# Linear attention feeding a squared-ReLU layer: two blocks of attention handled as one, and first blocks' steps at other places

## Chip, cores and metric

One core of one Trainium2 chip. The metric is the device time of one launch in microseconds (us), median of several runs of the same program; lower is better. TensorE is called PE, VectorE DVE, ScalarE ACT, GpSimd POOL, and SyncE SP; nearly all DMAs are issued from SP's queue.

## What is computed

Cut to what matters:

```python
# q, k, v, alpha: (4, 8, 768, 48)   w_in: (384, 2048)   w_out: (2048, 384)
for t in range(S):
    state = alpha[:, :, t, :, None] * state + einsum('bhd,bhe->bhde', k[:, :, t], v[:, :, t])
    y[:, :, t] = einsum('bhd,bhde->bhe', q[:, :, t], state)
x = y.transpose(0, 2, 1, 3).reshape(B * S, H * D)      # 3072 x 384
h = maximum(x @ w_in, 0)
out = (h * h) @ w_out
```

The first part is linear attention with a decay for each key feature, in sequence over 768 steps; the second is a feed-forward layer on its output. The weights come as 64-bit floats and are made into 32-bit ones on the chip.

## The kernel before

The sequence is cut into six chunks of 128 steps. A block is one chunk of one batch, so there are 24 blocks; block n has chunk n // 4 and batch n % 4. Four blocks make a group, and the 512 rows of x that a group gives go through the feed-forward layer together. Six groups are passed in turn (the program's g, 0 to 5), and while PE works on the layer of group g, the attention of group g + 1 is put in between.

**Attention of a block.** The logs of alpha (`ln`, on ACT) are summed along the chunk by a matmul with a triangular matrix (`cs`); from block 8 on the log is split on DVE into a high and a low part of fewer bits each (`sp`), so that this matmul runs in two fast passes. The exponentials of the sums and of their negatives (`eb`, `ei`, on ACT) scale q and k (`mq`, `mk`, on DVE). PE transposes both (`turn`, tile `T`), ACT copies them out of PSUM (`kc`, `qc`). Then `scores` (k with q, in two halves of 64 steps) and `state_sums` (k with v) write into the same two PSUM banks (tile `sckv`, lines L418 and L441). On DVE, `masked` copies the scores under a triangular mask into `am` (L426), `sums_copied` adds the old state to the first half's sums (`us`, L452), and `next_state` adds the second half's (L466) and multiplies by the last row of decays (L467). That row has to be turned from a row into a column: `bl` writes it to DRAM (`row<-b`), and `br` reads it back in two DMAs (`last<-row`). Output y is made in two parts, the first in `ga` (`yq` from states, and half of the masked scores), the second in `gb`; `ev` copies it out of PSUM to x.

**Pairs.** From block 4 on, work is placed by pairs n, n + 1. `PLAN` and `EARLY` (L996 to L1016) give each step of a pair a due time, in units of PE work, where 1.05 stands for six matmuls of 512 columns; `weave` (L1052) puts a step in front of the first piece of the layer that begins at or after its time. In `ga` of pair n: scores, sums, mask and us of block n, first part of y of pair n - 2, state step of block n. In `gb`: second part of y of pair n - 2, then scores, sums, mask, us and state step of block n + 1. Loads of later blocks are issued from the same plan, when the tile that they overwrite has been read. The table `AT` (L19) holds due times, scales and switches.

**The layer.** In group 0, and partly in group 1, it is computed with plain 32-bit matmuls (`h<-x,w_in`, `o<-w_out,hid`). After that each operand is split into a coarse part and a rest, and each product is made in three faster passes: in `in_x` the coarse one (`h<-xa,wb`) and the rests (`h<-xl,wl`), in `in_y`, two pieces later, a third with differences (`h<-xd,wd`). `in_post` makes the squared ReLU, `split_h` and `diff_h` split it for the second matmul. The split weights are made once (`prepare`), kept in DRAM, and streamed in again for every group (`pump`, as long as fewer than `room` tiles are in use). `split_x` and `diff_x` split the group's x, for each of three slices of 128 rows.

**The start.** An order written out by hand (`first`, L980 to L989) holds blocks 0 to 3, loads and weights among it. `warm` and `zeros` (L243, L380) are matmuls whose result nobody reads. `first0`, `middle0`, `second0` convert weight chunk 0 from 64 to 32 bits, on DVE (L174, L178), ACT (L187, L190) and DVE (L196, L200, L203). A word such as `gy0` holds the next load back until a mark has passed, here the first part of y of blocks 0 and 1.

All PSUM tiles come from one pool of eight banks. Every engine runs its own instructions in the order in which the program gives them.

Of the kernel before, what the change touches and what calls it, by code (L numbers as in the profile page):

```python
# [17 lines left out]
GB = 4  # L18
AT = {'u0': 2, 'evs': 0.4, 'lead': 4, 'post': 3, 'w_first': (45.82, 44.44, 94.99), 'wstep': 2.31, 'w_in_at': 1.92, 'w_in_by': 3.02, 'room1': 25, 'room': 26, 's0': 3, 'ahead': 12, 'late': 23, 'xs': 0.35, 'g0': (-0.17, 20.59, 27.02), 'sc0': (2.36, 2.26, 2.42), 'g1': (7.68, 18.74, 27.21), 'g': (2.3, 15.42), 'g1x': 47.42, 'gx': 39.86, 'g0x': 55.51, 'k0': 2, 'h0': 16, 'k1': 5, 'h1': 0, 'h1by': 5, 'evs0': 0.23, 'tp': 'DDAD', 'tp1': 'AADD', 'split': 8, 'o0': (42.39, 46.35), 'o1': (), 'o2': (21.54, 19.65, 30.49, 26.1, 43.38, 50.96), 'str1': 14.0, 'ga': 9.32, 'gb': 12.97}  # L19
# [6 lines left out]
def kernel(  # L26
# [37 lines left out]
    s_all = kept("s", B + 2, [128, NP, 64])  # L64
    u_all = kept("us", 3, [128, NP, 64])
    for t in s_all[0:B]:
        nc.gpsimd.memset(t, 0.0)
    s_t = [s_all.pop(0) for _ in range(B)]
    NV = 4
    tiles = {  # L70
        "a": kept("a_in", 2, [128, H * D]), "q": kept("q_in", 2, [128, H, 64]),
        "k": kept("k_in", 3, [128, H, 64]), "v": kept("v_in", NV, [128, H * D]),
    }
    for t in tiles["q"] + tiles["k"]:
        nc.gpsimd.memset(t[:, :, D:64], 0.0)

    NW = 8
    wt_pool = ctx.enter_context(tc.tile_pool(name="wt", bufs=26))
# [16 lines left out]
    for x, n in (("q", 2), ("q", 3), ("k", 3)):  # L95
        t = lent[x, n] = two_k("qk_lent", shape=(H, 64))
        nc.gpsimd.memset(t[:, :, D:64], 0.0)

    def tile_of(x, n):
        return lent.get((x, n), tiles[x][n % len(tiles[x])])  # L100
# [11 lines left out]
    marks, held = {}, []  # L112

# [12 lines left out]
    def load(n, xs="aqkv"):  # L126
        c, b = divmod(n, B)
        for x in xs:
            t = dense.get((x, n), tile_of(x, n))
# [62 lines left out]
    def convert_second(i):  # L192
# [10 lines left out]
        nc.vector.tensor_tensor(out=w, in0=w, in1=power.bitcast(FP32), op=ALU.mult)  # L203

# [27 lines left out]
    for t in s_all + u_all:  # L232
        nc.gpsimd.memset(t, 0.0)
# [4 lines left out]
    rows_t = [dram.tile([1, H * D], FP32, name=f"row{n}") for n in range(NBLK)]  # L238
# [4 lines left out]
    def warm(_):  # L243
        nc.tensor.matmul(
            out=ps_att.tile([128, NP, 64], FP32, tag="att", name="warm"),
            lhsT=s_t[0].rearrange("a p d -> a (p d)")[:, 0:128], rhs=s_t[0], start=True, stop=True,
        )

    for _ in range(3):
        warm(0)  # L250

# [13 lines left out]
    def ln(n):  # L265
        la = blk[n]["la"] = tile_of("a", n)
        nc.scalar.activation(out=la, in_=la, func=AF.Ln)

    SPLIT = AT["split"]

    def sp(n):
        if n < SPLIT:
            return
        la = blk[n].pop("la")
        hi = p2.tile([128, H * D], FP32R, tag="b", name="hi")
        lo = p2.tile([128, H * D], FP32R, tag="inv", name="lo")
        nc.vector.tensor_copy(out=hi, in_=la)
        nc.vector.tensor_tensor(out=lo, in0=la, in1=hi.bitcast(FP32), op=ALU.subtract)  # L280
        blk[n]["parts"] = hi, lo

    def cs(n):

        ps = blk[n]["cs"] = bank(n, "cs")
# [10 lines left out]

    def eb(n):
        if n < GB:
            b = blk[n]["b_wide"] = b_wide[n]
            b = blk[n]["b"] = b[:, :, 0:D]  # L300
            sums = sums_of_logs(n).rearrange("a (h d) -> a h d", h=H)
            nc.scalar.activation(out=b, in_=sums, func=AF.Exp)
            return
        b = p2.tile([128, H * D], FP32, tag="b", name="b")
        nc.scalar.activation(out=b, in_=sums_of_logs(n), func=AF.Exp)
        b = blk[n]["b"] = b.rearrange("a (h d) -> a h d", h=H)

    def ei(n):
        inv = blk[n]["inv"] = p2.tile([128, H * D], FP32, tag="inv", name="inv")
# [849 lines left out]
```

## Time and profile before

| | before |
|---|---|
| runs, median of 3 (lowest, highest) | 516.7 us (516.4, 516.85) |
| the profiled execution: span from first to last instruction | 514.6 us |
| granted TensorE clock | 1.00 |
| HBM read, written | 84.57 MB, 17.33 MB |
| DMA engines, mean share | 71% |

The page gives for the profiled execution its span; a launch's time has 2.1 us more in the median of the runs. In the rows of the profile L12 is line 12 of the kernel, "x24" a count, and `out<-in` names the tiles. Rows of the chain of waits give start, length and what; rows of the timeline give start, length, engine, line, operation, and in brackets the idle time in front of it with what ended it. Rows of groups give the busy time, a comma, the mean of one in ns, and then idle time in front. An instruction of 32-bit matmul stands as two records.

### The profile page before, as it was taken

Reading aid. Unit: us, or ns where it says so; the run is one execution under the profiler, and the core shown is the slowest. Engines: PE = TensorE matmul, PEld = TensorE weight load, DVE = VectorE, ACT = ScalarE, POOL = GpSimd, SP = SyncE. Lnnn points to the kernel's source line nnn. Section 1 sums busy time; section 2 is a strip of 40 time slices with the busy share of each in tenths; the row PEclk is TensorE's granted clock in tenths of the full one; section 3 lists DMA queues with packets and bytes.
Section 4 is the critical chain, followed back from the end, with each engine's and each line's share of the span. In section 5 each row is a group of like instructions: output and inputs, shape, how many; then the busy total and the mean of one; then the engine's idle time right before and its main releaser. Section 6 shows DMA issues by size and latency. Waiting matters only on the chain.

```text
span 514.6 us, 12773 instructions
## 1 busy us (share of the span) xinstructions
PE 508.3 (99%) x5166; PEld 404.6 (79%) x5166; DVE 377.0 (73%) x656; ACT 302.3 (59%) x627; POOL 6.0 (1%) x33
## 2 busy tenths in 40 slices
PE   8999999999999999999999999999999999999997
PEld 6884456669877679988888888888888888888996
DVE  3798899898789869886698286799275588274961
ACT  4789875677788576376764175855075663144520
POOL 4000000000000000000000000000000000000000
PEclk9999999999999999999999999999999999999999
DMA  9989867272797788799975678894775544789201
GB/s 171 226 238 269 233 177 226 33 224 101 267 238 199 189 188 234 263 330 222 241 187 154 209 220 229 222 225 146 227 221 168 186 128 151 214 277 401 88 0 63
DMA packets 144794, 102.73 MB, mean 200 GB/s; under 512 B 116560, under 2 KB 118240, under 8 KB 144736
## 3 DMA queue, kind: packets, MB, share of 16 engines
q1 hardware_dynamic: 144736, 101.92, 70.4%
q8 instruction: 41, 0.67, 0.6%
q14 instruction: 17, 0.14, 0.1%
HBM read 84.57 MB, written 17.33 MB: 198 GB/s over the span
## 4 chain that ended last, share of the span: by engine, by line
PE 96%; DMA 2%; SPq 1%; DVE 1%; issue 0%; ACT 0%; DVEq 0%; POOLq 0%
PE h L681 31%; PE o L760 22%; PE o L843 13%; PE h L931 8%; PE o L855 6%; PE y L398 4%; PE sckv L418 3%; PE T L529 2%; PE sckv L441 2%; PE cs L288 1%; DMA a_in<-in_alpha_dram 1%; PE zeros L384 1%; DMA last<-row 1%; PE cs L291 1%; SPq L333 1%; PE cs L292 1%
## 5 line engine op out<-in xcount | busy, mean ns | idle before, releaser
L696 ACT ACTIVATE hid<-h 128x512 f32<-128x512 f32 x56 | 33.7, 601 | 88.4 <-PE h L681 86.7
L681 PE MATMUL h<-xd,wd 128*128 128x512 f32 x240 | 68.4, 398 | 0.0
L681 PE MATMUL h<-xa,wb 128*128 128x512 f32 x240 | 67.8, 391 | 0.0
L681 PE MATMUL h<-xl,wl 128*128 128x512 f32 x240 | 67.6, 390 | 0.0
L594 DVE TENSOR_TENSOR hid<-h,hid 128x512 f32<-128x512 f32 x56 | 38.5, 689 | 33.9 <-PE h L681 33.6
L562 ACT COPY x<-y 32x256 f32<-32x256 f32 (+1 forms) x137 | 48.9, 365 | 8.7 <-PE y L398 6.4
L681 PEld LDWEIGHTS h<-xl,wl 128*128 128x128 f32 x240 | 45.0, 188 | 9.6
L681 PEld LDWEIGHTS h<-xa,wb 128*128 128x128 f32 x240 | 44.9, 188 | 9.4
L681 PEld LDWEIGHTS h<-xd,wd 128*128 128x128 f32 x240 | 43.7, 188 | 9.2
L760 PE MATMUL o<-w_out,hid 128*128 128x384 f32 x144 | 48.9, 492 | 0.0
L931 PE MATMUL h<-x,w_in 128*128 128x512 f32 (+1 forms) x120 | 43.0, 511 | 0.0
L655 ACT ACTIVATE ha<-hid 128x512 fp32r<-128x512 f32 x42 | 26.7, 638 | 26.1 <-DVE hx L656 12.8
L760 PEld LDWEIGHTS o<-w_out,hid 128*128 128x128 f32 x144 | 26.7, 190 | 17.2
L710 DVE SCALAR_TENSOR_TENSOR hid<-hid 128x512 f32<-128x512 f32 x56 | 37.8, 684 | 0.0
L931 PEld LDWEIGHTS h<-x,w_in 128*128 128x128 f32 x120 | 22.4, 190 | 16.9 <-issue 13.9
L855 PE MATMUL o<-hd,wd 128*128 128x512 f32 x144 | 33.4, 391 | 0.0
L656 DVE SCALAR_TENSOR_TENSOR hl<-ha,hid 128x512 fp32r<-128x512 f32 x42 | 28.8, 686 | 4.7 <-ACT ha L655 4.4
L855 PEld LDWEIGHTS o<-hd,wd 128*128 128x128 f32 x144 | 26.8, 188 | 6.1 <-ACT o L848 0.6
L594 DVE TENSOR_TENSOR hd<-ha,hl 128x512 fp32r<-128x512 f32 x42 | 29.1, 692 | 1.9
L843 PE MATMUL o<-hx,wb 128*128 128x512 f32 x72 | 28.4, 394 | 0.0
L843 PE MATMUL o<-hx,wl 128*128 128x512 f32 x72 | 28.0, 389 | 0.0
L843 PE MATMUL o<-ha,wb 128*128 128x512 f32 x72 | 28.0, 389 | 0.0
(130 smaller groups left out, 950.4 us busy)
## 6 DMA issues: line engine op xcount, KB each, us to landing
wd<-do SPq DMA_DIRECT2D x37, 384.0 KB
wl<-lo SPq DMA_DIRECT2D x34, 384.0 KB
wl<-li SPq DMA_DIRECT2D x32, 384.0 KB
wd<-di SPq DMA_DIRECT2D x32, 384.0 KB
raw<-in_moe_w_in_dram SPq DMA_DIRECT2D x8, 768.0 KB
raw<-in_moe_w_out_dram SPq DMA_DIRECT2D x8, 768.0 KB
v_in<-in_v_dram SPq DMA_DIRECT2D x24, 192.0 KB
a_in<-in_alpha_dram SPq DMA_DIRECT2D x22, 192.0 KB
```

The costliest lines, as they stand in the source:

```text
L398: ins = nc.tensor.matmul(out=ys[e][64 * half : 64 * half + D + G * e, m % 2, p // 2, t], lhsT=lhsT, rhs=rhs, start=(half, e) not in seen, ...
L562: copy(out=x[kk][to : to + m, t : t + 2], in_=blk[n]["y"][e][r : r + m, :, p // 2],)
L594: nc.vector.tensor_tensor(out=o, in0=x, in1=z, op=op)
L655: nc.scalar.activation(out=a, in_=x, func=AF.Copy, scale=NEAR * E)
L656: nc.vector.scalar_tensor_tensor(out=l, in0=a.bitcast(FP32), scalar=-1.0 / E, in1=x, op0=ALU.mult, op1=ALU.add)
L681: nc.tensor.matmul(out=acc["h", j], lhsT=here[w, "i", p][:, kk, jj * 128 : (jj + 1) * 128], rhs=x_parts[x][:, kk], start=start and kk == 0 ...
L696: nc.scalar.activation(out=hid[j], in_=x, func=AF.Copy, scale=E)
L710: nc.vector.scalar_tensor_tensor(out=h, in0=h, scalar=0.0, in1=h, op0=ALU.max, op1=ALU.mult)
L760: nc.tensor.matmul(out=acc[t][:, 0:DM], lhsT=lhs[:, t * C : (t + 1) * C], rhs=rhs, start=start, stop=stop, skip_group_check=True,)
L843: nc.tensor.matmul(out=acc[c], lhsT=by_parts(here[w, "o", p], jj, c), rhs=x, start=n == 0 and w == "b", stop=n == NJ - 1 and w == "l", ski ...
L855: nc.tensor.matmul(out=acc[c], lhsT=by_parts(here["d", "o", p], n % 2, c), rhs=h_diff[n], start=False, stop=last and n == NJ - 1, skip_gro ...
L931: nc.tensor.matmul(out=ps, lhsT=w[:, kk, c0 : c0 + 128], rhs=xT[g][kk][:, cols], start=(kk == 0), stop=(kk == KM - 1),)
```

## The change

For blocks 4 to 23 the steps of a pair work on tiles that hold both blocks, one instruction for both: log (`pair_ln`), split (`pair_sp`), scaling of k and q (`pair_mk`, `pair_mq`), the row to DRAM and back (`pair_bl`, `pair_br`), the mask (`pair_masked`), us and state (`pair_states`). Scores and sums of a pair have banks of their own: `ga` now makes the scores and masks of both blocks and the first part of y of the pair before, `gb` the sums of both, the second part of y, and then us and state of both. Blocks 0 to 3 start from a state of zero, and us is a copy there. In the sums the odd heads have 48 columns in place of 64. x is split in one operation over three slices in place of three. For groups with n under 16, the high part of the log is copied by ACT.

Moved or resized, without change of what is computed: the order of `first`; the due times in `PLAN` and `AT`; `EARLY` is gone; the squared ReLU comes two pieces after `in_x` (`post` 3 to 2) and the first splits of h at piece 6 (`lead` 4 to 6). Tiles for streamed weights: 26 to 25, `room` 26 to 27 from group 2 on. q, a: one tile of a pair where there were two single ones; k: two pairs for three; v: two pairs for four. `JOINED` is off, and `osb` has 'D' in both places, which is the way of before. The lines `needs` and `done` only assert an order while the program is built.

By kind, before to after: instructions of DVE that differ in form or number are masks of 256 (48 to 8) and of 512 (0 to 20), scaling of q and k of 384 (48 to 8) and of 768 (0 to 20), state work of 192 (64 to 12) and of 384 (0 to 26), low parts (16 of 384 to 8 of 768), high parts (16 of 384 to 4 of 768, and 4 of 768 on ACT), x splits (30 of 512 to 10 of 1536). On ACT the logs go from 24 of 384 to 4 of 384 and 10 of 768, and xa from 15 of 512 to 5 of 1536. Row DMAs go from 48 to 24. PE has three `warm` and twelve `zeros` before, thirteen `warm` and one `pad` of 8 columns after.

```diff
-    s_all = kept("s", B + 2, [128, NP, 64])
-    u_all = kept("us", 3, [128, NP, 64])
+    s_two = kept("s", B // 2 + 1, [128, 2, NP, 64])
+    u_two = kept("us", 1, [128, 2, NP, 64])[0]
...
-    wt_pool = ctx.enter_context(tc.tile_pool(name="wt", bufs=26))
+    wt_pool = ctx.enter_context(tc.tile_pool(name="wt", bufs=25))
...
+    def pair_ln(n):
+        la = both(pair_of("a", n))
+        nc.scalar.activation(out=la, in_=la, func=AF.Ln)
...
+    def pair_sp(n):
+        if n < SPLIT:
+            return
+        la = both(pair_of("a", n))
+        hi, lo = wide("bhi", FP32R), wide("ilo", FP32R)
+        if n < AT["hia"]:
+            nc.scalar.copy(out=both(hi), in_=la)
+        else:
+            nc.vector.tensor_copy(out=both(hi), in_=la)
+        nc.vector.tensor_tensor(out=both(lo), in0=la, in1=both(hi).bitcast(FP32), op=ALU.subtract)
...
+    def pair_br(n):
         if n // B < NCH - 1:
-            row = rows_t[n].rearrange("a (p e d) -> (a d) e p", e=2, d=D)
+            row = rows_t[n].rearrange("a (m p e d) -> (a d) e m p", m=2, e=2, d=D)
             for e in range(2):
-                nc.sync.dma_start(out=last_t[n % 4][64 * e : 64 * e + D, :], in_=row[:, e])
+                nc.sync.dma_start(
+                    out=last[64 * e : 64 * e + D, n % 4 : n % 4 + 2, :], in_=row[:, e]
+                )
...
+    def pair_masked(n):
+        ps = two.pop(("s", n))
+        for e in range(2):
+            nc.vector.copy_predicated(
+                out=am_t[n // 2 % NAM][:, e].rearrange("a p t -> a (p t)").rearrange("a (p t) -> a p t", t=64),
+                data=ps[e].rearrange("a m p t -> a (m p) t"),
+                mask=halves_mask.bitcast(U32).unsqueeze(1).to_broadcast([128, 2 * NP, 64]),
+            )
...
+    def pair_states(n):
+        ps, i = two.pop(("k", n)), n % B // 2
+        old = s_two[i]
+        nc.vector.tensor_tensor(out=all_own(u_two), in0=all_own(ps[0]), in1=all_own(old), op=ALU.add)
...
+        if len(ps) > 1:
+            s_two[i], spare = spare, old
+            s = all_own(s_two[i])
+            by = rows_of(last)[:, n % 4 : n % 4 + 2, :].unsqueeze(3).to_broadcast([64 + D, 2, NP, D])
+            nc.vector.tensor_tensor(out=s, in0=all_own(ps[1]), in1=all_own(u_two), op=ALU.add)
+            nc.vector.tensor_tensor(out=s, in0=s, in1=by, op=ALU.mult)
...
+    def ga(a, n, t):
...
         if n is not None:
-            for f in (scores, state_sums, masked, sums_copied):
-                f(n)
+            pair_scores(n)
+            pair_masked(n)
         if a is not None:
-            product = y_begin(a)
...
+            y_first(a)
-        if n is not None:
-            next_state(n)
...
+    def gb(a, n, t):
...
+        if n is not None:
+            pair_sums(n)
         if a is not None:
-            product, passed = two.pop("y")
...
+            y_second(a)
         if n is not None:
-            for f in (scores, state_sums, masked, sums_copied, next_state):
-                f(n + 1)
+            pair_states(n)
...
-    def split_x(g, kk):
...
-        split_to(x_parts["a"][:, kk], x_parts["l"][:, kk], x_parts["x"][kk])
+    def split_x(g):
...
+        split_to(flat(x_parts["a"]), flat(x_parts["l"]), flat(x_parts["x"]))
...
     first = """
-        zeros2 ln0 cs0 ln1 eb0 cs1 load0v ei0 mq0 mk0 load2a eb1 qT0 load3a qc0 mq1
-        kT0 kc0 load1v ei1 qT1 mk1 load2k load2q qc1 sc0 kT1 weights0 kc1 kv0 load3q
-        am0 lt1 sc1 ln2 us0 ln3 cs2 lt0 am1 load3k kv1 cs3 eb2 us1 ei2 gt1 mk2
-        load2v weights1 ya0 mq2 yb0 lc1 gy0 eb3 kT2 lc0 load3v qT2 ei3 load4a zeros2
-        st0 ea00 kc2 qc2 ed01 ed02 first0 zeros2 load4q mq3 zeros2 mk3 qT3 middle0
-        qc3 kT3 second0 first1 kc3 lt3 lt2 sc2 kv2 am2 ea03 us2 sc3 kv3 gk3 middle1
-        weights2 lc3 am3 us3 ha0 ya2 yb2 second1 weights3 ea20 lc2 ed21 ha1 ha3
-        weights4 ed22 ed23 first2 st2 middle2 ha2 hb0 load4v hb1 st3 st1 load4k
+        load1v warm0 warm0 load0v ln0 cs0 ln1 warm0 ei0 eb0 cs1 warm0 mq0 mk0 load2a
+        weights0 qT0 load3a kT0 eb1 mq1 ei1 warm0 mk1 kc0 qc0 kT1 qT1 kc1 sc0 qc1 kv0 sc1
+        lt1 ln2 load2k cs2 am1 load2q lc1 kv1 gt1 am0 warm0 ln3 load3q warm0 us0 cs3 ei2
+        first0 us1 ya0 yb0 lt0 eb2 eb3 ei3 st1 mk2 mq2 ea00 load3k kT2 kc2 warm0 lc0 load2v
+        mq3 qT2 ed02 gy0 weights1 load3v middle0 lt2 st0 lt3 mk3 qT3 kT3 warm0 warm0 lc2
+        qc2 sc2 kc3 qc3 ed01 second0 first1 ea03 load4q middle1 kv2 load4k weights2 am2 us2
+        sc3 kv3 am3 us3 gk3 lc3 load4a second1 ha0 weights3 ya2 yb2 ea20 ed21 ed22 ha1 ed23
+        first2 middle2 ha3 st3 ha2 load4v hb1 hb0 weights4 st2
     """
...
     PLAN = (
-        (-1.2, "ln0 ln1"),
-        (-0.5, "sp0"),
-        (0.0, "sp1"),
-        (2.5, "cs0 cs1 eb0 ei0"),
+        (-0.48, "pair_ln"),
+        (-0.27, "pair_sp"),
+        (2.08, "cs0 cs1 eb0 ei0"),
...
-        (9.5, "ga"),
-        (10.5, "gb"),
+        (9.56, "ga"),
+        (10.29, "gb"),
     )
```

In groups 2 to 5 the due times of `ga` and `gb` come from `AT`: 9.32 and 12.97 before, 9.84 and 13.76 after.

More of the change, by code (lines that the diff above doesn't have):

```diff
@@ L423, in masked @@
     def masked(n):
+        done("am", n)
         ps = two[n]
@@ L435, in state_sums @@
     def state_sums(n):
+        needs("k", n)
+        needs("load v", n)
+        done("kv", n)
         ps = two[n]
@@ L776, in out_plain @@
     def out_plain(p, t, pieces):
+        needs("w", NW + p)
         if p == 0:
@@ L927, in ffn_in @@
         w, c0 = w_in[j * NW // NJ], j % (NJ // NW) * 128
+        needs("w", j * NW // NJ)
+        needs("x", *(GB * g + i // C for i in range(cols.start, cols.stop, 2 * C)))
         n = cols.stop - cols.start
```

393 lines of the change are left out of this document (253 added, 140 removed).

## The prediction

> **What bounds the kernel now.** I read the page's busy shares first, then the chain of work that ended last, then the stages.
>
> ```profile
> span 514.6 us, 12773 instructions
> PE 508.3 (99%) x5166; PEld 404.6 (79%) x5166; DVE 377.0 (73%) x656; ACT 302.3 (59%) x627; POOL 6.0 (1%) x33
> PE 96%; DMA 2%; SPq 1%; DVE 1%; issue 0%; ACT 0%; DVEq 0%; POOLq 0%
> ```
>
> PE is never idle to speak of, and the chain is PE from end to end. So the time is what PE executes, plus the few places where it is held back. All other engines matter only where they make PE late. The stages (start and length, then busy time by engine) say who could:
>
> ```profile
> 0.00:26.20 26.20, 24.15 (x438) 18.94 (x438) 15.37 (x33) 16.04 (x32) 5.99 (x33) 1.00 1.01 197
> 26.20:76.90 50.70, 50.59 (x393) 29.18 (x386) 44.62 (x78) 42.73 (x82) 0.00 (x0) 1.00 0.86 231
> 124.50:164.00 39.50, 39.49 (x346) 32.12 (x344) 34.72 (x60) 30.54 (x59) 0.00 (x0) 1.00 0.77 220
> ```
>
> Third in each row is DVE: 44.62 of 50.70 and 34.72 of 39.50 us, 88%. In the first 26 us the DMA share is 1.01 and PE is filled with idle matmuls, so the start is not PE's. Where PE is held back I read off the chain, by comparing equal pieces of work (start, length, what):
>
> ```profile
> 18.92 3.89 PE zeros L384 x18
> ...
> 143.69 0.90 PE T L529 x24
> 144.60 0.46 PE T L529 x8
> ...
> 162.91 1.15 PE T L529 x32
> ...
> 168.13 0.62 PE sckv L418 x32
> ...
> 170.30 0.79 PE y L398 x31
> 171.09 2.78 PE o L760 x8
> ...
> 181.48 0.77 PE T L529 x16
> 182.25 0.71 PE T L529 x16
> ...
> 187.03 0.62 PE sckv L418 x32
> ...
> 189.52 4.37 PE o L760 x24
> ...
> 256.30 0.89 PE h L681 x3
> ...
> 261.29 0.62 PE y L398 x31
> 261.91 0.46 PE sckv L418 x32
> ...
> 262.83 17.91 PE o L843 x78
> ...
> 444.94 32.64 PE h L681 x144
> ```
>
> A turn of a pair takes 1.15 us at 162.91, but 1.36 at 143.69 and 1.48 at 181.48: 0.21 and 0.33 lost. Scores, sums and first y together take 189.52 - 187.03 = 2.49, but 171.09 - 168.13 = 2.96 at 168.13: 0.47 lost. The fourth place shows its cause in the timeline:
>
> ```profile
> 237.04 0.36 DVE L467 TENSOR_TENSOR s<-s,last 128x192 f32<-128x192 f32 x1 [3.61 <-DMA last<-row]
> ...
> 237.61 0.69 PE L398 MATMUL y<-am,v_in 64*48 64x64 f32 x32
> ...
> 238.66 0.63 PE L418 MATMUL sckv<-qs,ks 48*64 48x64 f32 x27 [0.24 <-DVE hid L594]
> ...
> 239.73 0.53 PEld L681 LDWEIGHTS h<-xd,wd 128*128 128x128 f32 x3
> ```
>
> The state step in `ga` stood 3.61 us on DVE for the row that the DMA had not brought; the hid operations behind it came late, their PSUM bank was not free, and the second part took 239.73 - 237.61 = 2.12 us against 262.83 - 261.29 = 1.54: 0.58 lost. Sum of the four: 0.21 + 0.33 + 0.47 + 0.58 = 1.59 us.
>
> **The change, part by part.** *PE's work.* The matmuls of the computation are the same in number and, but for some with 48 columns in place of 64, in shape. What can differ is how often PE goes over from 128-row matmuls to 64-row attention work and back. Such a visit has a price: scores after y take 0.46 (261.91), after a large matmul 0.62 (187.03), so 0.16 going in; three h matmuls after a visit take 0.89 (256.30) against 3 x 32.64/144 = 0.68, so 0.21 coming out. That is 0.37 a visit. The order of PE's instructions has 35 visits from the first h matmul on before and 34 after (the sums of blocks 4 and 5 now stand directly behind their scores): -0.37 us.
>
> *Pair operations on DVE.* The rows (mean ns of one behind the comma):
>
> ```profile
> L426 DVE COPY_PREDICATED am<-halves_mask,sckv 128x256 f32<-128x256 uint32 x48 | 18.7, 443 | 11.0 <-PE sckv L441 9.3 <-issue 1.7
> L314 DVE TENSOR_TENSOR k_in<-k_in,inv 128x384 f32<-128x384 f32 x20 | 11.1, 556 | 4.4 <-ACT inv L310 4.4
> L656 DVE SCALAR_TENSOR_TENSOR xl<-xa,x 128x512 fp32r<-128x512 f32 x15 | 9.5, 683 | 0.0
> L203 DVE TENSOR_TENSOR w_in<-w_in,power 128x768 f32<-128x768 f32 x8 | 7.7, 958 | 0.3
> L467 DVE TENSOR_TENSOR s<-s,last 128x192 f32<-128x192 f32 x20 | 7.2, 358 | 10.7 <-DMA last<-row 10.0
> ```
>
> Sizes 192, 384, 512 and 768 cost 358, 556, 683 and 958 ns, about 1.04 ns an element and 160 ns fixed; a 1536 is then some 1,760 by extrapolation. Scaling q and k: 40 x 556 becomes 20 x 958, 22.2 to 19.2 us. Splitting x: 30 x 683 becomes 10 x 1,760, 20.5 to 17.6. State sums and steps: 64 of 192 become 12 of 192 and 26 of 384, 22.9 to 18.8. Log split: the 16 low parts of 384 become 8 of 768 (8.9 to 7.7), and of the high copies four pairs go to ACT and four stay; I count nothing for those. Masks: 40 x 443 become 20 of 512, between 20 x 683 = 13.7 and 2 x 443 x 20 = 17.7; I take 14, nearer the row of that size, from 17.7. In all 3.0 + 2.9 + 4.1 + 1.2 + 3.7 = 15 us less of DVE's 377. ACT loses as many calls on logs and x as it gains copies. None of this is on PE's chain: by itself it is worth nothing, and only the 1.59 us above can come back through it.
>
> *The state step moves from `ga` to `gb`, with half as many row DMAs* (48 become 24). The wait for the row then begins some 4 units of work later, about 5 us (a unit of 1.05 is six h matmuls, 6 x 0.227 us). The 3.61 us wait at 237.04 is covered by that; if the row is later still, the same hid operations are behind it. Scores now leave their two banks at the mask and do not hold them until the state step. So the 0.58 should go, and part of the other three. Bounds: 0 and 1.59. I take 1.2, the one with its cause named and two thirds of the rest.
>
> *New tightness.* From log to cumulative sum it was 3.7 units, now 2.56, about 3.3 us, for a log, a high copy and a low part of 768, three times about 0.96 = 2.9. If ACT is late by more than 0.4 us, cs waits and PE with it. A 1,760 ns operation can also hold a bank for 1.1 us longer than three of 683 with something between. At ten pairs the bounds are 0 and ten times one 512 operation beyond the slack, 10 x (0.68 - 0.4) = 2.8; I take 0.2, since the stages from 212 us on have DVE and ACT far from full. SP waits for one q, a, k and v buffer per pair where it had the same number of single ones, which changes nothing there; the weight tiles go from 26 to 25, while `room` goes to 27, so SP stands longer at weight loads with row and k loads behind it. That is in the same 0.2.
>
> *The start.* The fillers are 15 matmuls before and 14 after, but the block of 18 records (3.89 us at 18.92) is gone. What sets the start is this:
>
> ```profile
> 15.26 0.36 DVE L452 TENSOR_TENSOR us<-sckv,s 128x192 f32<-128x192 f32 x1 [1.11 <-PE sckv L441]
> ...
> 17.92 0.74 SPq L122 DMA_DIRECT2D raw<-in_moe_w_in_dram  x1
> ...
> 20.00 0.54 DVE L174 TENSOR_SCALAR power<-raw 128x768 uint32<-128x768 uint32 x1
> ...
> 29.80 0.96 DVE L203 TENSOR_TENSOR w_in<-w_in,power 128x768 f32<-128x768 f32 x1
> ...
> 29.93 2.42 PE L931 MATMUL h<-x,w_in 128*128 128x256 f32 x10
> ```
>
> Weight chunk 1 is converted at 30.76, and the second of the h matmuls from 29.93 on (1.3 us each) needs it at 31.2: nothing that leaves chunk 1 where it is gains more than 0.5 us. Its load at 17.92 now has the hold (`gy0`) itself, so it begins behind the first part of y of blocks 0 and 1. In front of that y stands, new on DVE, the first conversion of chunk 0, between the two copies to `us`. Chunk 0's load stands three loads of 192 KB earlier. At 197 GB/s the nine loads in front of it and itself (2.5 MB) take 12.7 us; from some 2.3 us on that is 15.0, about when DVE comes to it (15.26). Then two operations of 0.54 put y 1 us later and chunk 1's load at about 18.5, while the six loads of blocks 2 and 3 behind it still keep the DMA engines full; chunk 1 lands no later. Two state operations (2 x 0.36) now precede it on DVE. Bounds: -1.4 (fillers of 3.89 gone, 0.5 from chunk 1 and 0.9 if DVE idles less) and +1.7 (y's 1.0 and the 0.72 in full). I take -0.2: the ends are alike far, and the row at 29.93 shows PE there waiting for nothing, so a small part of the filler's room can be had.
>
> Sum against the profiled execution: 514.6 - 0.37 - 1.2 + 0.2 - 0.2 = 513.0. The median of the runs is 516.7, 2.1 above that span, for what lies around it, which the change leaves: **515.1 us**.
>
> **Rivals.** *No gain, the change not doing what it says* (0.16): the stalls come back elsewhere, since 15 us less leave DVE near the 88% of the two stages; 516.7 less the 0.37 is 516.3. For it: only four losses stand out in the whole run, each at another kind of work. Against it: the largest has its cause shown.
>
> *Slower through chunk 0* (0.14): DVE executes in order, and the copy to `us` waits behind the conversion of chunk 0. If chunk 0 lands when DVE touched it before, 20.00, `us` comes at 21.4 and no longer at 15.62, chunk 1's load begins 4.7 us later than 17.92 and its conversion ends at 35.4, with PE needing it at 31.2: +4.2, so 519.4. It decides from a landing after about 17: each us beyond costs one. Against it: three fewer loads stand in front.
>
> *PE goes slow in the start* (0.03): the first fillers run at half pace.
>
> ```profile
> L384 PE MATMUL zeros<-s x24: 379/379/634, 3.8 to 22.4; 128*128 128x256 f32 x24
> ```
>
> Duration minimum, median, maximum: 634 at first, 379 later. With the 18 records gone, PE may stand idle from 19 to 22 us and begin the h matmuls at that pace: six of them, 1.49 us, would take 3.0; +1.5 and 516.7. By the Trainium skill (TensorE: Matmul & The Clock Gate, What's actually happening) the array's clock falls to half after an idle window of about 3.4 us, and comes back after a busy one; by that rule the loss would be at most 1.7 us. Single fillers remain in that stretch, which speaks against it.
>
> *A larger gain* (0.07): start and stalls both at their bounds, 514.6 - 0.37 - 1.59 - 1.4 = 511.2, so 513.3.
>
> **How the numbers follow.** The forecast has 0.60, from 514.0 to 516.2: its stalls between 0.6 and 1.59, its start between -0.7 and +0.7. About 0.2% (1.0 us) is what a measurement can tell from no change: faster below 515.7, slower above 517.7. Faster: three quarters of the forecast (0.45), all of the larger gain (0.07) and a third of no gain (0.05), 0.57. Slower: the 0.14 and 0.03 for the tightness at its bound, 0.17. The same: 0.26. The range is 513.0 to 518.0 and leaves out half of the larger gain and two thirds of the slower rival.
>
> **What would show it.** Right: no wait of DVE for `last<-row` over 1 us; turns of 1.15 us throughout; DVE busy near 362 us; h matmuls without a break from about 30 us. Wrong: PE waiting at cs for ACT or DVE; h at 30 us beginning later than 31; the first conversion of chunk 0 on DVE preceded by idle time of over 2 us; large matmuls held by a bank behind the 1536 operations.

## The result, and the profile after

The changed kernel takes 514.61 us (median of 7 runs, 514.06 to 515.8) where the kernel before took 516.7 (7 runs beside it, 516.16 to 517.76): a ratio of 0.996, with a 95% interval of 0.9948 to 0.9971. The forecast was 515.1 us, with a range of 513.0 to 518.0. The change is 0.4% faster, clear of the 0.2% that a measurement can tell from nothing.

The page of the changed kernel's profiled execution (514.06 us; its span, busy time by engine, and the chain by engine):

```profile
span 512.3 us, 12578 instructions
PE 505.1 (99%) x5164; PEld 402.5 (79%) x5164; DVE 371.5 (73%) x550; ACT 304.3 (59%) x611; POOL 5.6 (1%) x27
PE 94%; DVE 2%; SPq 2%; DMA 1%; issue 0%; ACT 0%; DVEq 0%; POOLq 0%
```

The span is 2.3 us shorter, and PE's busy time 3.2. DVE has 106 operations fewer and is busy for 5.5 us less. The same stages as in the prediction, with their new bounds (start and length, busy time of PE, PEld, DVE, ACT, POOL, clock, DMA share, GB/s):

```profile
0.00:25.87 25.87, 22.94 (x436) 17.56 (x437) 15.40 (x35) 14.73 (x30) 5.55 (x27) 1.00 1.01 201
25.87:76.05 50.18, 49.60 (x389) 28.78 (x385) 43.77 (x69) 45.22 (x87) 0.00 (x0) 1.00 0.83 228
123.95:163.30 39.35, 39.35 (x345) 32.09 (x343) 34.61 (x45) 33.09 (x61) 0.00 (x0) 1.00 0.82 240
```

DVE is as full in these stages as it was: 34.61 of 39.35 us is 88% again. Where PE was held before, the chain of the changed kernel shows (start, length, what):

```profile
30.03 16.99 PE h L1090 x60
...
139.06 1.15 PE T L681 x32
...
167.44 1.09 PE sc L553 x64
168.53 1.40 PE y L465 x92
169.93 2.78 PE o L913 x8
...
181.59 1.15 PE T L681 x31
...
238.16 1.01 PE kv L580 x56
...
239.69 2.28 PE h L834 x9
...
442.64 32.64 PE h L834 x144
```

The turns that took 1.36 and 1.48 us take 1.15. Scores and first part of y take 169.93 - 167.44 = 2.49 (2.96 before, with the sums), and the second part with the sums 239.69 - 238.16 = 1.53 (2.12). The last layer begins at 442.64 in place of 444.94. To see where the 2.3 us came from, the start of the large matmul behind the first n (h and o; 1,776 records in each kernel) is set against its twin. At these points both kernels have done the same large matmuls and the same attention:

```
 n      before   after   difference
   40    37.58    37.40   -0.18
  120    76.69    76.05   -0.64
  280   128.03   127.48   -0.55
  520   202.41   200.95   -1.46
  640   228.84   227.32   -1.52
  760   267.88   265.63   -2.25
 1760   507.95   505.65   -2.30
```

So 0.18 comes from the start, 0.46 from the first attention of the big pairs (blocks 4 and 5), 0.9 from the stretch with the two turns and the y at 168, 0.7 from the place at 237, and nothing from the last 240 us.

### The profile page after: what moved, and what is told of

Its sections match the earlier page's. It is cut to its first block, busy times and chain, and to the rows that moved or that the text cites. A ratio compares the mean times of both kernels' runs of the same rounds, so it can differ in the third digit from the quotient of the medians.

```text
span 512.3 us, 12578 instructions
## 1 busy us (share of the span) xinstructions
PE 505.1 (99%) x5164; PEld 402.5 (79%) x5164; DVE 371.5 (73%) x550; ACT 304.3 (59%) x611; POOL 5.6 (1%) x27
## 4 chain that ended last, share of the span: by engine, by line
PE 94%; DVE 2%; SPq 2%; DMA 1%; issue 0%; ACT 0%; DVEq 0%; POOLq 0%
PE h L834 33%; PE o L913 22%; PE o L1000 13%; PE h L1090 8%; PE o L1012 6%; PE y L465 5%; PE T L681 2%; PE sc L553 2%; PE kv L580 2%; SPq L134 2%; DMA a_lent<-in_alpha_dram 1%; PE cs L327 1%; PE cs L330 1%; PE cs L331 1%; DVE am L494 0%
## 5 line engine op out<-in xcount | busy, mean ns | idle before, releaser
L714 ACT COPY x<-y 32x256 f32<-32x256 f32 (+2 forms) x137 | 48.6, 366 | 22.8 <-PE y L465 20.5
L810 DVE SCALAR_TENSOR_TENSOR hx<-hx,hid 128x512 fp32r<-128x512 f32 x36 | 24.7, 685 | 7.9 <-ACT hx L809 7.9
L851 ACT ACTIVATE h<-h 128x512 f32<-128x512 f32 x24 | 14.0, 584 | 24.7 <-PE h L834 24.6
```

Source lines behind the costliest of these rows:

```text
L714: copy(out=x[kk][to : to + m, t : t + 2], in_=blk[n]["y"][e][r : r + m, :, p // 2],)
L810: nc.vector.scalar_tensor_tensor(out=l, in0=a.bitcast(FP32), scalar=-1.0 / E, in1=x, op0=ALU.mult, op1=ALU.add)
```

## The experiments

Two explanations were on the table: *places* (each loss has one operation behind it that stands too late or too early, and the change moved it) and *load* (pair operations take work off DVE, and that lets PE run). All ratios are against the kernel before, run beside them on the same chip.

**The pair operations of DVE alone.** Every DVE operation for a pair is taken apart again; places, queues and DMAs stay.

```
 # changed kernel, one of six places
-        t = pair_of(x, n)[:, :, :, 0:D]
-        nc.vector.tensor_tensor(out=t, in0=t, in1=factor.rearrange("a m (h d) -> a m h d", h=H), op=ALU.mult)
+        for m in range(2):
+            t = pair_of(x, n)[:, m, :, 0:D]
+            nc.vector.tensor_tensor(out=t, in0=t, in1=heads_of(factor[:, m]), op=ALU.mult)
```

> The changed kernel with its places, queues and DMAs as they are, but every DVE operation for a pair taken apart again into one for each block (masks, scaling of q and k, state sums and steps, low parts of the logs) and, for x, three of 512 in place of one of 1536. Theory 'places': the operations stand early enough also when they are single; turns stay at 1.15, the span stays between 512.1 and 512.8, ratio to before 0.996, while DVE's busy time goes back up by 5 us or more. Theory 'load': with DVE's work as before the losses at the turns and second parts come back, span 513.5 to 514.6, ratio 0.998 to 1.000.

Ratio 0.9952 (0.9937 to 0.9966), span 512.4, all turns 1.15. The page of this run against the changed kernel's:

```profile
PE 505.6 (99%) x5164; PEld 402.8 (79%) x5164; DVE 376.6 (74%) x644; ACT 304.1 (59%) x611; POOL 5.5 (1%) x27
```

With 94 operations more, DVE is busy for 5.1 us more, nearly what it was before the change, and the time is the same. Taking work off DVE in this form is worth nothing here; *load* falls. The run also shows how much the merging saves. Groups of the changed kernel by shape (busy time, mean ns of one):

```profile
L563 DVE COPY_PREDICATED am<-halves_mask,sc 128x512 f32<-128x512 uint32 x20 | 13.6, 735 | 0.2 <-PE sc L553 0.2
L373 DVE TENSOR_TENSOR k_in<-k_in,inv 128x768 f32<-128x768 f32 x10 | 9.6, 958 | 7.4 <-ACT inv L352 7.4
L810 DVE SCALAR_TENSOR_TENSOR xl<-xa,x 128x1536 fp32r<-128x1536 f32 x5 | 8.8, 1755 | 17.9 <-ACT xa L809 17.9
```

and the same work taken apart:

```profile
L566 DVE COPY_PREDICATED am<-halves_mask,sc 128x256 f32<-128x256 uint32 x40 | 14.3, 438 | 0.2 <-PE sc L555 0.2
L377 DVE TENSOR_TENSOR k_in<-k_in,inv 128x384 f32<-128x384 f32 x20 | 10.6, 554 | 4.4 <-ACT inv L355 4.4
L834 DVE SCALAR_TENSOR_TENSOR xl<-xa,x 128x512 fp32r<-128x512 f32 x15 | 9.5, 684 | 17.8 <-ACT xa L832 17.8
```

By durations, 40 masks of 438 ns are 17.5 us; the engine was busy with them for 14.3, because the records of neighbouring operations overlap. An operation saved is worth 5.1 us / 94 = 54 ns here, a third of the 160 ns of fixed part that its duration shows. The Trainium skill (Vector Engine (DVE) Microarchitecture Reference, Measured stream behaviour on trn2) gives, for streams of 32-bit integers, about 75 ns per instruction after queue overlap beside a slope of 1.04 ns per column; this case's 54 ns, on 32-bit floats, is on that side and not on the side of the 160.

**The wait for the row alone, in the kernel before.** Only the multiplication that waited 3.61 us for the row moves, from the end of `ga` to the start of `gb`.

```
 # kernel before, in gb
+            by_last(n)      # s = s * last, taken out of next_state(n) in ga
             for f in (scores, state_sums, masked, sums_copied, next_state, by_last):
                 f(n + 1)
```

> The kernel before, with one operation moved: the multiplication of the first block's state by the row (`last`), which stood at the end of `ga`, stands at the start of `gb`; everything else is as before. Theory 'places' (each loss of PE has one late operation behind it): DVE no longer waits over 1 us for last<-row in front of the hid operations at 237, the second part there takes 1.54 us in place of 2.12, and the other three losses (turns at 143.7 and 181.5, first y at 168) stay: span 514.0, ratio to before 0.999. Theory 'load' (DVE has too much to do for PE in these stages, and the losses come back somewhere as long as it has): the loss at 237 turns up within the next few us, span 514.6, ratio 1.000.

Ratio 1.0012 (1.0001 to 1.0023), span 515.3. The chain of this run, at the place that lost 0.58 and at a new one:

```profile
237.84 0.62 PE y L398 x31
...
239.39 4.32 PE h L686 x18
...
321.58 0.37 ACT x L567
321.99 1.66 PE h L686 x6
```

The second part takes 239.39 - 237.84 = 1.55: the row was the cause of this loss, and moving one operation takes it away. But at 321 us an h matmul now waits 0.93 us for ACT's copies of y. In the kernel before the same copies run from 318.10 to 323.19 us, later still, and no h waits for them; so h probably stands in another bank there, which was not followed further. 85 us behind the edit the gain is given back. *Places* was right for the loss and wrong in the sum.

**Scaling earlier, in the kernel before.** Of the two slow turns, the one at 143.69 waited for the second q of the pair on DVE. The expectation takes the other, at 181.48, for the same, but the timeline of the kernel before shows another cause there:

```profile
144.00 0.55 DVE L314 TENSOR_TENSOR q_in<-q_in,b 128x384 f32<-128x384 f32 x1
...
144.60 0.46 PE L529 MATMUL T<-ident,q_in 64*128 64x64 f32 x8
...
179.64 2.56 ACT L562 COPY x<-y 16x256 f32<-16x256 f32 x7
...
182.25 0.46 PE L529 MATMUL T<-ident,k_in 64*128 64x64 f32 x8
```

At 144.60 PE goes on with q when DVE has scaled it (144.55). At 182.25 it goes on with the second block's k, just behind the last of ACT's copies of y (182.20); its k had been scaled at 181.51 and its q at 181.98. A copy of y reads PSUM and writes x, so what it can give a turn is only a bank. The edit below moves the scaling alone.

```
 # kernel before
-        (3.5, "mk0"), (4.0, "bl0"), (4.5, "mq0 mk1 bl1"), (5.0, "mq1"),
+        (3.3, "mk0"), (3.5, "mk1"), (3.7, "mq0"), (3.9, "mq1"), (4.0, "bl0"), (4.5, "bl1"),
```

> The kernel before, with the scaling of k and q of each pair 0.2 to 1.1 units earlier (3.3, 3.5, 3.7, 3.9 in place of 3.5, 4.5, 4.5, 5.0) and nothing else. Theory 'places': the two turns that took 1.36 and 1.48 us waited for the second q of the pair, scaled by DVE at 144.00 and 181.43 in the middle of the turn; both become 1.15, the hold at 237 (0.58) and the loss at 168 (0.47) stay: span 514.1, ratio 0.999. Theory 'load': DVE does the same work, something else is late by as much; span 514.6, ratio 1.000.

Ratio 1.0068 (1.0048 to 1.0089): both expectations wrong. The turn at 143 is cured (1.15), the one at 181 is not, and the turn at 87.57, 1.15 before, now takes 2.00, 0.64 of it a wait for q. The timeline of this run at 181 (start, length, operation, in brackets the idle time and what ended it):

```profile
181.44 0.56 DVE L314 TENSOR_TENSOR k_in<-k_in,inv 128x384 f32<-128x384 f32 x1 [2.66 <-DMA k_in<-in_k_dram]
...
184.88 0.43 PE L529 MATMUL T<-ident,k_in 64*128 64x64 f32 x7 [2.47 <-DVE us L452]
```

The earlier place asks for k before its load has landed; DVE stands 2.66 us in front of everything queued behind, and PE 2.47, for a bank that `us` reads. An operation can be too early as well as too late.

**New times without the pairs, and pairs without the new times.** In the first kernel the kernel before gets the due times, room and other numbers of the changed one; in the second the changed kernel gets the old ones.

```
 # first: kernel before with AT, and PLAN as (3.13, "mk0 mk1"), (4.43, "mq0 mq1"), (6.75, "turn") ...
 # second: changed kernel with the old AT, and PLAN as
+        (4.0, "pair_mk"), (4.5, "pair_bl"), (4.75, "pair_mq"), (6.5, "turn"), (7.0, "kc1 qc1 pair_br"), ...
```

> The kernel before, single blocks and its own start, with the due times, room and other numbers of the changed kernel (k at 3.13, q at 4.43, turn at 6.75, ga 9.84, gb 13.76, groups at 3.4 and 16.07). Theory 'times': the four losses go, 1.59 of 2.3 us come without any pair: span 512.7 to 513.4, ratio 0.996 to 0.998. Theory 'structure': the state step in `ga` still waits for the row and single blocks keep four operations where there was one, span 514.3 or more, ratio 0.9995 or more.

> The changed kernel with all its pair tiles, pair operations and the new start, but with the due times, room and other numbers of the kernel before (pair_ln -1.2, pair_mk 4.0, pair_mq 4.75, turn 6.5, pair_br 7.0, ga 9.32, gb 12.97, groups at 2.3 and 15.42). Theory 'times' (what went away are late operations, and the new due times are what makes them early): losses at turns and second parts come back, 0.6 to 1.9 us, span 513.0 to 514.2, ratio 0.997 to 0.999. Theory 'structure' (scores of both blocks in one visit, sums and step behind the second part): span within 0.4 of 512.3, ratio 0.996.

New times alone: 1.0002 (0.9993 to 1.001), span 514.1. Old times with pairs: 1.014 (1.0125 to 1.0155), span 521.9. Each half alone gains nothing or loses; together they are 0.996. In the first kernel all turns take 1.15 to 1.17 and the second part at 239 us 1.54, so these losses of before are cured by times; but it pays elsewhere. Its timeline in front of the cumulative sums of blocks 8 and 9:

```profile
155.98 0.35 DVE L279 CAST hi<-a_in 128x384 fp32r<-128x384 f32 x1
...
156.37 0.56 DVE L280 TENSOR_TENSOR lo<-a_in,hi 128x384 fp32r<-128x384 f32 x1
...
156.98 0.44 PE L292 MATMUL cs<-lo,causal_r 128*128 128x384 f32 x1
```

The last low part ends at 156.93 and cs waits for it: the four cs matmuls take from 156.07 to 157.26, 1.19 us, where four of 0.18 are 0.71. That is the tightness from log to cumulative sum, real here, and absent in the changed kernel. (ACT makes the high copies there, but that is not the reason, as the run with high copies on DVE shows.) It also keeps the one extra visit of PE. In the second kernel the turn is late for another reason; its timeline:

```profile
226.76 0.96 DVE L373 TENSOR_TENSOR k_in<-k_in,inv 128x768 f32<-128x768 f32 x1 [1.87 <-ACT inv L352]
...
229.57 0.95 DVE L373 TENSOR_TENSOR q_in<-q_in,b 128x768 f32<-128x768 f32 x1
...
230.58 0.46 PE L681 MATMUL T<-ident,q_in 64*128 64x64 f32 x8 [0.76 <-DVE q_in L373]
```

One operation for both blocks is done only when both are done: the turn of the first block now waits for the second one's q. Turns of 1.31 to 2.41 us at eight pairs make 5.5 of the 9.6 us that this span is longer than the changed kernel's; in the longest, at 181, PE waits 0.8 for ACT's copies of y, as in the kernel before. Two more waits make 2.9: an o matmul waits 1.8 for DVE's `osb`, and a cs 1.1 for a low part. The pair operation needs the earlier due time (4.43 before a turn at 6.75), and the old times (4.75 and 6.5) do not give it.

**Sums and state step back in `ga`.**

```
 # changed kernel
     ga: pair_scores, pair_masked, + pair_sums, y_first, + pair_states
     gb: - pair_sums, y_second, - pair_states
```

> The changed kernel with state sums and state step of the pair back in `ga` (sums behind the scores, step behind the first part of y) in place of `gb`. Theory 'places': the wait of DVE for last<-row comes back, in some pairs by 1 to 4 us, with hid operations behind it, and PE loses 0.3 to 0.6 us at one to three of them: span 512.8 to 513.6, ratio 0.997 to 0.998. Theory 'load', and also a third one, that two reads of a row in place of four are alone enough to bring it in time: no wait over 1 us, span 512.3, ratio 0.996.

Ratio 1.0416 (1.0394 to 1.0438): far worse than either theory, and no wait for the row over 1 us is in it. Its timeline at one pair:

```profile
191.86 1.16 PE L553 MATMUL sc<-qs,ks 48*64 48x64 f32 x64
...
192.84 1.09 PE L580 MATMUL kv<-v_in,k_in 64*64 64x48 f32 x64
...
195.71 1.32 DVE L563 COPY_PREDICATED am<-halves_mask,sc 128x512 f32<-128x512 uint32 x2
196.48 0.31 PE L465 MATMUL y<-qs,s 48*48 48x64 f32 x2 [2.55 <-DVE am L563]
```

The y matmuls read nothing of these masks: they belong to the pair before. What a mask of this pair can give them is only a PSUM bank, that of its scores, and y goes on as each of the two masks ends. Of the eight banks the second layer holds four for its sums of o; two of scores and two of sums fill the rest, and y has none until the mask, which stands behind hx and hd operations on DVE, is done. So `gb` is not only where the row has come; beside the four banks of o it is the only one of the two places where the sums of a pair fit. These waits are 9.8 of the 19.6 us that the span is longer; 2.5 are holds without a releaser, and some 5 the clock (0.990 in the mean over 531.9 us), both taken up below. (The rival that two reads of a row in place of four bring it in time stays possible: it came in time here, but PE was late too.)

**The price of a visit.** The sums and the state step get a visit of their own, 1.2 units behind `gb`: nine visits more.

```
 # changed kernel
-    gb: pair_sums, y_second, pair_states
+    gb: y_second           # and gc, at gb + 1.2: pair_sums, pair_states, loads of v and k
```

> The changed kernel with state sums and state step of a pair taken out of `gb` and put 1.2 units behind it, between the large matmuls, as a visit of their own: nine more changes between 128-row and 64-row work in PE's order, the same matmuls. Theory 'price' (0.37 us for each visit of PE to 64-row work, 0.16 in and 0.21 out): 9 x 0.37 = 3.3, span 515.6, ratio to before 1.002. Theory 'hidden' (the going over costs only where the neighbour is already late): span 512.3 to 513.0, ratio 0.996 to 0.997.

Ratio 1.0084 (1.0062 to 1.0106), span 518.3: 6.0 us more than the changed kernel. Set against the changed kernel at the same large matmuls, seven of the nine places cost 0.35 to 0.37 each; that is the 0.37 of the prediction. The other two cost 1.5, where the sums wait 0.54 us for a bank that ACT's `inv` reads and the large matmuls behind them run late as well. That makes 5.5 of the 6.0; 0.3 more comes at 192.6 us, where nothing was moved, in front of PE's 4,546th instruction (see below). *Price* was right, and too small by the waits.

**The start.** Three kernels, each with one edit of the order written out for the first blocks:

```
 # old order: the words of the kernel before, with st1 behind st0
 # chunk 0 later:   first0 us1 ya0 yb0          ->  us1 first0 ya0 yb0
 # chunk 1 later:   first1 ... middle1 ... am2 us2 sc3 kv3 am3 us3  ->  ... am2 us2 sc3 kv3 am3 us3 first1 middle1
```

> The changed kernel with the order of the first blocks' steps of the kernel before (with its fillers; the state step of block 1 earlier, before the sums of block 3, because the pair shares a buffer). My reading of the two traces: the first h without a break begins at 30.0 us in both, so the new order of the start is worth nothing: span 512.3, between 511.9 and 512.8, ratio 0.996. Rival: the new start only came out even because pair tiles made the old order worse (one k tile more in the pair buffers, loads at other places): span 513 to 514.5, ratio 0.998.

> The changed kernel with the first conversion of chunk 0 on DVE behind the second copy to `us` in place of before it. My prediction feared that this conversion holds the copy and with it y and the load of chunk 1. In the trace the copy stood at 15.75 us, 1.0 us after the conversion began. Theory 'chunk 0 in front costs': y of blocks 0 and 1 begins 1.0 us earlier (16.1), the load of chunk 1 at 17.3, the unbroken h matmuls 0.3 to 1.0 us earlier, span 511.3 to 512.0, ratio 0.994 to 0.9955. Theory 'DVE sets the start' (the chain of waits runs through DVE from 19.6 to 28.3 us, behind all that): span 512.2 to 512.6, ratio 0.996.

> The changed kernel with the first conversion of chunk 1 (two operations, 1.1 us on DVE) behind the masks and copies of blocks 2 and 3 in place of before them. Theory 'DVE sets the start': y of blocks 2 and 3 begins 1.0 us earlier (26.3), and chunk 1 is ready 1 us later (about 32), so the h matmuls begin earlier and then wait for chunk 1; the span moves by -0.5 to +0.3 from 512.3, ratio 0.995 to 0.997. Theory 'chunk 1 sets the start': all of the 1 us appears, span 513.0 to 513.4, ratio 0.9975.

The start of the changed kernel, by its timeline:

```profile
14.80 0.56 DVE L189 TENSOR_SCALAR power<-raw 128x768 uint32<-128x768 uint32 x1 [0.17 <-DMA raw<-in_moe_w_in_dram]
...
15.75 0.35 DVE L532 COPY us<-sckv 112x192 f32<-112x192 f32 x1
...
18.33 0.37 SPq L134 DMA_DIRECT2D raw<-in_moe_w_in_dram  x1
...
28.28 0.46 PE L465 MATMUL y<-qs,us 48*48 48x64 f32 x16 [0.45 <-DVE us L532]
```

Chunk 0 landed at about 14.8, 0.17 us after DVE came to it, near the 15.0 worked out in the prediction. With chunk 0 later: ratio 0.9959 (0.9944 to 0.9974), and the large matmuls are 0.09 us ahead of the changed kernel's; y of blocks 0 and 1 begins at 16.99 in place of 17.12 and not 1 us earlier, because a cumulative sum that waits for an alpha load stands ahead of it on PE. The conversion in front of `us` costs 0.1 us and no more, and the slow rival through chunk 0 had no ground. With chunk 1 later: 0.9965 (0.9951 to 0.9979), y of blocks 2 and 3 goes through without a wait at 27.22, and then

```profile
31.57 1.75 PE L1090 MATMUL h<-x,w_in 128*128 128x256 f32 x7 [0.81 <-DVE w_in L218]
```

h waits 0.81 us for chunk 1, and at the 40th large matmul this kernel is 0.28 behind the changed one. The two ends of the start are in balance: what one gains the other loses. With the old order: 0.9997 (0.9983 to 1.0012), 0.41 us behind the changed kernel at the 40th large matmul, so the expectation that the new order is worth nothing was wrong: it is worth 0.4 within the new structure, and against the start of before 0.18. The other 1.1 us of this run is not the start's.

**A loss without a releaser, and ACT's high copies.** That 1.1 us, in the old-order run on PE:

```profile
190.55 0.33 PE L913 MATMUL o<-wb,ha 128*128 128x384 f32 x1
191.87 0.34 PE L913 MATMUL o<-wl,hl 128*128 128x384 f32 x1 [0.99 <-issue]
```

"issue" means that PE waited for nothing that the profile shows. The last kernel tests the tight step from log to cumulative sum, and whether this loss comes back in a kernel with another edit:

```
 # changed kernel
-'hia': 16
+'hia': 8        # high copies of pairs 8 to 15 on DVE, not ACT
```

> The changed kernel with the high copies of the logs of four pairs (8 to 15) on DVE in place of ACT: four more operations of 0.56 us on DVE, four fewer of 0.84 on ACT, in the two stages where DVE was 88% busy. It is the single step of the change that gives DVE's work away to ACT. Theory 'tight' (2.6 units from log to cumulative sum are only enough because ACT makes the high copy): cs waits for DVE at one to three pairs by 0.3 to 1.0 each, span 512.8 to 514.0, ratio 0.997 to 0.9995. Theory 'slack' (DVE's own high copy is 0.28 us shorter, and DVE has room): no wait at cs, span 512.2 to 512.6, ratio 0.995 to 0.997. Apart from both: four variants of the changed kernel lost 0.2 to 1.0 us without a releaser near 191 us, in the weights of the second layer, where the profiled execution of the changed kernel lost nothing; if that belongs to the place and not to the variant, this one shows it too, and its span has that much more.

Ratio 0.9967 (0.9953 to 0.9981), span 513.5, no wait at cs: *slack* is right, DVE has room for four copies more. And the loss is there again:

```profile
191.22 0.34 PE L913 MATMUL o<-wb,ha 128*128 128x384 f32 x1
192.50 0.45 PE L913 MATMUL o<-wl,hl 128*128 128x384 f32 x1 [0.94 <-issue]
```

Counting PE's instructions in the trace settles its place. In five variants of the changed kernel the loss lies between the 4,545th and the 4,546th, and in the kernel before (the y at 168 us) and its row variant between the 3,777th and the 3,778th. These are three times 256 apart. The page lists 41 reads of the instruction queue with 0.67 MB, 16 KB each, for some 10,490 instructions of PE, which is one read for 256. The trace's DMA records give their starts (held: the time between two starts of PE beyond the usual one):

```
 kernel                 count    held   read begun   PE goes on   between
 before                  3777    0.34     167.93       170.30       2.36
 row later               3777    0.33     168.22       170.52       2.30
 chunk 0 later           4545    0.46     189.04       191.38       2.34
 old order               4545    1.15     189.48       191.87       2.39
 single operations       4545    0.35     189.22       191.77       2.55
 chunk 1 later           4545    0.37     189.26       191.83       2.57
 high copies on DVE      4545    1.10     189.88       192.50       2.62
 changed                 4545    0.00     188.71       191.02       2.31
```

PE goes on 2.3 to 2.6 us after the read begins, whatever the loss: it stands for its own instructions. The other traces agree. The 14th and the 17th read stand in this table, and 3,777 and 4,545 are 14 and 17 times 256, plus 193. In all fourteen traces PE never passes such a count less than 2.30 us after the read of that number began; and the two holds without a releaser in the run with sums back in `ga`, 2.12 and 0.38 us, stand at 5,569 and 7,361, the counts of the 21st and 28th read. The visits make this possible, since a 64-row matmul and its weight load are two instructions in 14 to 17 ns. Why a read begins late was not followed. Each row is one execution. In the changed kernel's own the read was just in time; its seven executions have spans from 512.3 to 514.0, so this one was the luckiest, which fits a loss of 0 to 1.1 us there.

**Fewer visits.** If a visit costs 0.35, the turn can ride along with `ga` and `gb`; the code has a switch for it.

```
 # changed kernel
-'joined': 0, ...   (3.13, "pair_mk"), (4.43, "pair_mq")
+'joined': 1, 'g0': (3.39, 12.7, 25.2, 35.9), ...   (7.3, "pair_mk"), (7.8, "pair_mq")
```

> The changed kernel with the turn of one block in `ga` and of the other in `gb`, one pair ahead of the scores (`joined` 1; scaling of k and q at 7.3 and 7.8, four steps in the first group), so that PE goes over to 64-row work 31 times in place of 38, with the same matmuls. Theory 'price': 7 x 0.35 = 2.5 us less, span 509.8 to 510.8, ratio 0.991 to 0.993. Rival 'banks and times': four banks of T beside those of scores, sums and y, and due times that nobody has fitted to it, hold PE by more than is saved: span 512.5 to 518, ratio 0.997 to 1.007.

Ratio 1.1131 (1.1103 to 1.1158). The waits of PE in this run (total us, times, longest):

```profile
PE y L465 <- DVE am L563: 22.6, 9, 5.8
PE kv L580 <- ACT qs L689: 6.5, 7, 1.2
```

Both expectations were far too small. It is the banks again: two more of T in each visit, and y waits for masks that it does not read. PE is idle for 45.2 us in place of 7.2; and the granted clock is 0.952 in the mean over 576.8 us, which is another 28 us of the 64.5 that the span is longer (see the last section). A visit is cheap beside a bank that is not free. None of the twelve kernels is faster than the changed one by more than the intervals.

## Why the prediction was right

*The bound.* PE is the bound in both, and the change works only through PE's visits and the places where PE is held. The run with single operations shows this outright.

*Visits, -0.37.* Right. The stretch with the sums of blocks 4 and 5 (the 40th to the 120th large matmul), in which other steps moved too, is 0.46 shorter, and the price is 0.35 to 0.37 where it was measured by itself.

*Four stalls, -1.2 of 1.59.* All 1.59 came back, so the term was too small by 0.4, and its reasons were right in part. The row caused the 0.58, as said: moving one multiplication cures it. "Part of the other three" through freed score banks was not shown at any of them. The turn at 143 waited for the scaling of the second q, and moving the scaling cures it. The turn at 181 did wait for a bank, but for one that ACT's copies of y were reading. Both take 1.15 in the kernel with new times and no pairs, so times alone cure them; which of the times does it at 181 was not separated. The 0.47 at 168 us was, for 0.34 of it, PE waiting for its instructions. That belongs to neither kernel's design, as five variants of the changed kernel have such a loss at 191 us: that the changed kernel's own profiled execution has none was luck. So the profiled difference of 2.3 us flatters the change somewhat, and the medians, 2.1 apart, are the better number.

*DVE, 15 us less.* The step that was mis-sized: 5.5 us, with 371.5 us busy and not the 362 named as a sign of being right. The sum took durations as if they added up; back to back, an operation saved is worth 54 ns and not 160. Part by part the durations were right (958 ns for 768 elements as taken, 1,755 where 1,760 was taken from a line through smaller sizes, 735 for a mask where 700 was taken). It did no harm, since the prediction gave it no worth by itself.

*New tightness, +0.2.* It measured 0 in the changed kernel. The mechanism is real, 0.48 us at one cs in the kernel before with the new times, but even four more copies on DVE did not bring it out in the changed one.

*The start, -0.2.* Measured -0.18 at the 40th large matmul. Chunk 0 landed at about 14.8 (15.0 worked out), y came 1.2 us later (1.0), and the load of chunk 1 was issued at 18.33 (18.5). The match for y is luck: with the conversion out of its way y comes only 0.13 us earlier, and what holds it is the cumulative sum that the new order puts ahead of it on PE.

*The rivals.* "No gain" fell, as the change is 2.1 us faster; but the new times without pairs do gain nothing, and the pair operations with the old times lose 1.4%. Chunk 0 was in time, and its conversion in front of `us` cost 0.1 us. PE did not go slow in the start: the granted clock is 1.00 there.

## What to carry to other kernels

Where one engine is the bound from end to end, take other work away only if its lateness shows as a hold of that engine; 94 operations and 5.1 us of busy time less on DVE were worth nothing here. An operation merged over two blocks is ready only when both are: the merge needs its own due times, and neither the old structure with the new times nor the new one with the old times gains. Before a hold is put down to the code, see whether it lies at the same count of instructions in other variants; then it can be the engine's own instruction supply, and its length changes from one variant to the next (0 to 1.15 us here at one count).

## What was not expected of the hardware

A hold costs more than its length. In the run with sums back in `ga`, PE stood from 193.9 to 196.5 us; the columns are those of the stages above, the granted clock third from the end:

```profile
193.50:196.40 2.90, 0.43 (x28) 0.30 (x20) 2.76 (x6) 1.32 (x3) 0.00 (x0) 1.00 1.01 239
196.40:199.00 2.60, 2.23 (x89) 2.08 (x92) 0.91 (x3) 0.00 (x0) 0.00 (x0) 0.73 0.06 20
199.00:202.00 3.00, 3.00 (x29) 2.88 (x22) 2.90 (x6) 0.00 (x0) 0.00 (x0) 0.67 0.00 0
202.00:205.00 3.00, 3.00 (x47) 2.75 (x46) 2.93 (x5) 0.00 (x0) 0.00 (x0) 1.00 0.45 131
```

The clock is 0.73 and 0.67 in the next 5.6 us, a loss of 2.6 x 0.27 + 3.0 x 0.33 = 1.7 us on top. In the run with scaling earlier the hold of 2.47 us is followed by 0.75 and 0.68 over 6 us, and in the run with fewer visits the clock falls several times, once behind a hold of only 1.56 us that ends at 185.6 (0.51 from 187.3 to 190.8). This is the clock rival's mechanism, in other places than feared: holds under 1.3 us, as in the kernel before and the changed one, did not bring it about. No single length decides, for two holds stayed at 1.00: 2.12 us at 247 in the run with sums back in `ga`, and 1.81 us at 208 in the run with pairs and old times. The Trainium skill (TensorE: Matmul & The Clock Gate, What's actually happening) has the clock fall after an idle window of about 3.4 us that runs free; here holds of 1.56 to 2.9 us were enough, and the loss at 196 us is of the size that the prediction took from that page, 1.7 us.
